# An adaLN transformer block: k-times-v product placed between q products, row sums as two rounded matmuls, three more unread matmuls in the opening

## The chip, the cores and the metric

The kernel runs on one NeuronCore of a Trainium2 chip. The metric is the device time of one execution in microseconds; the median of several executions is compared. A profile is one execution recorded by the hardware profiler.

The engines carry these names in the profile: PE is TensorE (PEld its weight loads), DVE is VectorE, ACT is ScalarE, POOL is GpSimd, and SP issues the DMAs.

## The reference

The input is `x` of 2048 rows by 512 columns, in float32. One row `c` of 512 makes six modulation vectors. A linear-attention block and a bilinear gated block follow, each on a normalised and modulated input and each added back with a gate.

```python
mod = (silu(c) @ w_mod).reshape(1, 6, 1, 512)
sa, ca, ga, sb, cb, gb = six rows of mod
h = layernorm(x) * (1 + ca) + sa
q, k, v = h @ wqkv, 32 heads of 16
pq, pk = phi(q), phi(k)                    # phi(t) = (t > 0 ? t + 1 : exp(t)) + 1e-6
kv = sum over s of pk[s] (outer) v[s]      # one 16 x 16 block per head
z  = sum over s of pk[s]
o  = (pq @ kv) / (pq . z + 1e-6)
x  = x + ga * (o @ wo)
h  = layernorm(x) * (1 + cb) + sb
x  = x + gb * (((h @ w_gate) * (h @ w_up)) @ w_down)
```

## The kernel before

**Precision.** A product of two float32 matrices is made of three matmuls in the type F32R: each operand is split into a rounded high part (a copy on ScalarE) and the rest as a low part (a subtraction on VectorE or GpSimd), and high x high, high x low and low x high are added in PSUM. `split` and `split_raw` make the parts (lines 192 to 194), `product` issues the three matmuls (lines 206, 207 and 208).

**Order.** The schedule is written by hand: each engine gets its instructions in the order in which the code calls them. The 2048 rows are 16 token tiles of 128 rows, in four chunks of four. PSUM has four accumulator banks (`acc_bank`) and four working banks (`bank`); a working bank is given to a new tile when its last reader is done with it.

**The opening (to about 27 us).** The first chunk of `x` is loaded, its statistics are taken, the tiles are normalised and transposed (`transpose_token`, line 278), and two modulation vectors are computed. `keep_on(n)` (line 153) issues n matmuls into the bank `ps_idle` that nobody reads; 18 stand at the start and 2 between the transposes of token tiles 0 and 1. `block_pe` (line 388) and `block_one` (line 399) are the small sums of the modulation.

**k tiles (27 to 129 us).** For each token tile i a loop makes a k product (`proj(i + 2, wk)`), its phi, its split, and adds its products with the normalised input into the four accumulators `tacc` (`t_tile`, lines 355 to 357). `zacc` adds up phi(k) over the tiles on VectorE (`z_add`, line 340). The table `extra` puts further work behind single tiles: the splits of the v weights `wv`, the modulation vectors (`mod_part`, lines 169 and 171; `mod_col`, line 176; `mod_row`, line 186), the loads and splits of `wo`. `mod_row` sums a vector over the 128 partitions and spreads the sum over all rows: one F32 matmul with a 128 x 128 matrix of ones. It is called behind tile 11 (row 2, `ga`) and behind tile 15 (row 5, `gb`). In tile 15 the same matmul makes `zb` from `zacc` (line 654).

**The turn (125 to 157 us).** The accumulators are turned into kv. The eight steps on VectorE are, for each of four k: `n` (line 739), then the low part (line 194), with the high part on ScalarE between them. Then 48 matmuls of 128 columns multiply the v weights with them:

```python
kvps = bank()
for g in range(KD):
    a, b = g * P, (g + 1) * P
    product(kvps[:, a:b], [(cut(wv[k], a, b), cut(tt[k], a, b)) for k in range(KD)])
```

Around them stand q products (`proj(i, wq)`, 12 matmuls of 512 columns each), whose phi is `q_a` (two ScalarE steps, lines 310 and 311) and `q_b` (a maximum and addition on VectorE, line 314). The result is masked to the heads' blocks (line 757), split, and multiplied with `wo` in `w_out` (four groups of three matmuls; the product with `ga` is line 725, and its split follows). Beside it run the denominators: `den_p` (phi(q) times zb, line 676, on POOL or VectorE), `den_r` (sum over a head, line 682), `den_b` (addition and reciprocal, lines 691 and 692), `den_c` (scaling of phi(q), line 711).

**y and the second block (157 us to the end).** `turn_a(i)` transposes the scaled phi(q) (line 782), `turn_h` and `turn_l` split it (lines 786 and 790), and `y_a` multiplies it with the combined weights (line 807). The second block then runs as a stream of matmuls (lines 970 and 1048 to 1050).

Of the kernel before, what the change touches and what calls it, by code (L numbers as in the profile page):

```python
# [8 lines left out]
F32 = mybir.dt.float32  # L9
# [13 lines left out]
def tile_adaln_block(  # L23
# [50 lines left out]
    def B(tag, shape=(P, D), dt=F32):  # L74

        return T(tiles, tag, shape, dt)
# [4 lines left out]
    def bank():  # L81
        return T(ps_w, "bank")
# [1 line left out]

    ident = consts.tile([P, P], F32, name="ident")
    make_identity(nc, ident)
    ones = consts.tile([P, P], F32, name="ones")
    nc.gpsimd.memset(ones, 1.0)
    mask = consts.tile([P, P], F32, name="mask")
    nc.gpsimd.memset(mask, 1.0)  # L90
    m3 = mask.rearrange("p (b i) -> p b i", i=DH)
# [16 lines left out]
    def load(src, tag):  # L108
        raw = B(tag, (P, *src.shape[1:]))[:src.shape[0]]
        nc.sync.dma_start(raw, src)  # L110
        return raw
# [47 lines left out]
    def silu():  # L159
        nc.scalar.activation(ce, ct, AF.Exp, scale=-1.0)  # L160
        nc.vector.tensor_scalar(ce, ce, 1.0, None, op0=ALU.add)
        nc.vector.reciprocal(ce, ce)
        nc.vector.tensor_mul(sc, ct, ce)
# [9 lines left out]
    def mod_col(acc, ps):  # L173

        for b in range(KD):
            nc.tensor.matmul(ps[:, b:b + 1], acc[:, b * P:(b + 1) * P], ones[:, 0:1], start=True, stop=True)
        return ps

    def col_out(v, ps, add):
        t = consts.tile([P, KD], F32, name=f"col{v}")  # L180
        nc.vector.tensor_scalar(t, ps[:, :KD], add, None, op0=ALU.add)
        return t

    def mod_row(v, acc):
        ps = bank()
        nc.tensor.matmul(ps, ones, acc, start=True, stop=True)
        t = consts.tile([P, D], F32, name=f"row{v}")
        nc.scalar.activation(t, ps, AF.Copy)
        return t


    def split(src, h, l, low=None):
        nc.scalar.activation(h, src, AF.Copy)
        (low or nc.vector).tensor_tensor(l, src, f32(h), op=ALU.subtract)

    def split_raw(raw, shape=(P, D), low=None):
        h = B("w", shape, F32R)
        l = B("w", shape, F32R)
        split(raw, h[:raw.shape[0]], l[:raw.shape[0]], low)
        return h, l  # L200

    def product(ps, pairs):

        n = len(pairs)
        for i, ((ah, al), (bh, bl)) in enumerate(pairs):
            nc.tensor.matmul(ps, ah, bh, start=i == 0, stop=False)  # L206
            nc.tensor.matmul(ps, ah, bl, start=False, stop=False)  # L207
            nc.tensor.matmul(ps, al, bh, start=False, stop=i == n - 1)  # L208

    def product2(pss, pairs):  # L210

# [10 lines left out]
    def cut(pair, a, b):  # L222
        return pair[0][:, a:b], pair[1][:, a:b]
# [77 lines left out]
    def proj(i, w, of=bank):  # L301

        ch, j = divmod(i, NJ)
        ps = of()
        product(ps, [(cut(norm[ch].t[k], j * P, (j + 1) * P), w[k]) for k in range(KD)])
        return ps
# [29 lines left out]
    def z_add(i):  # L336
        if i == 1:
            nc.vector.tensor_tensor(zacc, phk[0], phk[1], op=ALU.add)
        elif i > 1:
            nc.vector.tensor_tensor(zacc, zacc, phk[i], op=ALU.add)  # L340
        phk.pop(i - 1, None)
# [22 lines left out]
    def q_b(i):  # L364
        phi_b(q_ps.pop(i), phq[i])
# [16 lines left out]
    def sums_in(b):  # L382
        return ps_idle if b == 1 else ps_m

    def block_pe(v, b):
        at, ps = at_of(v, b), sums_in(b)
        for k, raw in enumerate(half_of(v, b)):
            nc.tensor.matmul(ps[:, at:at + 1], raw, sc[:, k:k + 1], start=k == 0, stop=k == KD - 1)
# [3 lines left out]
    def half_dve(v, half, *ks):  # L392
        if 0 in ks:
            sums[v, half] = B("f")[:, :D // 2]
        mod_acc(sums[v, half], [raw_half[v, half][k // 2][:, k % 2] for k in range(KD)], ks)

    def block_one(v, b):
        at = at_of(v, b)
        nc.tensor.matmul(sums_in(b)[:, at:at + 1], sums[v, b // 2][:, b % 2 * P:(b % 2 + 1) * P], ones[:, 0:1],
                         start=True, stop=True)  # L400

    def block_out(b):
# [38 lines left out]

    keep_on(18)
    n0.stats(0)
    silu()
    n0.stats(1)
    n0.rstd_of(0, 2)
# [10 lines left out]
    keep_on(2)  # L457
    n0.transpose_token(1)
    block_pe(1, 0)
    half_dve(0, 0, 0, 1, 2, 3)  # L460
    weight_h(0)
    n0.transpose_token(2)
    n0.transpose_token(3)
    block_one(0, 0)
    block_out(0)
    weight_l(0)
# [77 lines left out]
    def mod_load(*vs):  # L544
        raw_m.update({v: load_mod(v) for v in vs})

    def mod_part(v, *ks):
        if 0 in ks:
            accs[v] = B("f")
        mod_acc(accs[v], raw_m[v], ks)  # L550
# [4 lines left out]
             7: lambda: (wv.extend(split_raw(r) for r in raw_v[3:4]),),  # L555
             8: lambda: (mod_part(2, 0, 1), mod_load(3)),
             9: lambda: (mod_part(2, 2, 3), mod_load(4)),
             10: lambda: (mod_part(3, 0, 1, 2), mod_load(5)),
             11: lambda: (mod_part(3, 3), mod_part(4, 0, 1), rows.update({2: mod_row(2, accs[2])})),
             12: lambda: (raw_o.extend(load(wo_v[k], "raw") for k in range(KD)), mod_part(4, 2, 3), cols.update({3: col_out(3, mod_col(accs[3], bank()), 0.0)})),  # L560
             13: lambda: (mod_part(5, 0, 1, 2), cols.update({4: col_out(4, mod_col(accs[4], bank()), 1.0)})),
             14: lambda: (mod_part(5, 3), wo_s.extend(split_raw(x) for x in raw_o)), 15: lambda: rows.update({5: mod_row(5, accs[5])})}
    q_at = {4: 3}
    ahead = {}

# [46 lines left out]
    for i in range(4, NT):  # L612
        ch, j = divmod(i, NJ)
        more = ch + 1 < NCH
        if i > 1:
            ahead[i + 2] = proj(i + 2, wk) if i + 2 < NT else proj(i + 6 - NT, wq)
        if i in q_at:
            qps = proj(q_at[i], wq)
        if i + 1 < NT:
            k_split_x(i + 1)  # L620
        if i + 1 < NT:
            k_split(i + 1)
        if more and j < 2:
            t_tile(i, 0, 1)
            nx.transpose(2 * j, 2 * j + 1)
            nx.modulated(ca, sa, 2 * j, 2 * j + 1, cast=nc.vector)
            norm[ch + 1:] = [nx]
        if ch + 2 < NCH and j == 1:
            nx2 = Norm(xts[ch + 2])
            nx2.stats(0, 1)  # L630
        if ch + 2 < NCH and j == 2:
            nx2.stats(2, 3)
            nx2.rstd_of()
        if ch + 2 < NCH and j == 3:
            nx = nx2
            nx.xhat(2)
        if i + 2 < NT:
            k_phi(i + 2, ahead.pop(i + 2))
        else:
            q_a(i + 6 - NT, ahead.pop(i + 2))  # L640
            q_b(i + 6 - NT)
        if i in q_at:
            q_a(q_at[i], qps)
            q_b(q_at[i])
        if i + 1 < NT:
            z_add(i + 1)
        if ch + 2 < NCH and j == 2:
            nx2.nmr_of()
            nx2.xhat(0, 1)
        if ch + 2 < NCH and j == 3:  # L650
            nx.xhat(3)
        if i == NT - 1:
            zps = bank()
            nc.tensor.matmul(zps, ones, zacc, start=True, stop=True)
            zb = consts.tile([P, D], F32, name="zb")
            nc.scalar.activation(zb, zps, AF.Identity, bias=eps_z)  # L656
        t_tile(i, *range(2 if more and j < 2 else 0, KD))
        if i in extra:
            extra[i]()
# [24 lines left out]
    def den_a(ch, *js, on=None):  # L684

        for j in js:
            den_p(ch, j, on=on)
            den_r(ch, j)
# [44 lines left out]
    den_a(0, 0, 1, on=nc.vector)  # L733
    ps = proj(6, wq)
    fs, tt = [], []
    for k in range(KD):
        f = B("n")
        nc.scalar.activation(f, tacc[k], AF.Copy, scale=ca[:, k:k + 1])
        nc.vector.scalar_tensor_tensor(f, zb, sa[:, k:k + 1], f, op0=ALU.mult, op1=ALU.add)
        fs.append(f)  # L740
    for f in fs:
        tt.append((B("w", dt=F32R), B("w", dt=F32R)))
        split(f, *tt[-1])
    q_a(6, ps)
    q_tile(7)
    kvps = bank()
    for g in range(KD):
        a, b = g * P, (g + 1) * P
        product(kvps[:, a:b], [(cut(wv[k], a, b), cut(tt[k], a, b)) for k in range(KD)])
    q_b(6)  # L750
    q_b(7)
    den_p(1, 2)
    den_a(0, 2, on=nc.vector)
    ps = proj(8, wq)
    kvp = (B("xh", dt=F32R), B("xl", dt=F32R))
    kvf = B("n")
    nc.vector.tensor_tensor(kvf.rearrange("p (g c) -> p g c", g=KD), kvps.rearrange("p (g c) -> p g c", g=KD),
                            mask.unsqueeze(1).to_broadcast([P, KD, P]), op=ALU.mult)
    den_p(0, 3, on=nc.vector)
    split(kvf, *kvp)  # L760
    den_r(0, 3)
    den_b(0)
    q_a(8, ps)
    ps = proj(9, wq)
    q_b(8)
    w_out(0, 1)
    q_a(9, ps)
    den_c(0, 1)
    w_out(2, 3)
    q_b(9)  # L770
    q_tile(10)


    pqs = {}
# [322 lines left out]
        return [lambda: den_p(ch, j)], [lambda: den_r(ch, j)]  # L1097

    turn_a(0)
    ps = proj(11, wq)  # L1100
    turn_h(0)
    turn_l(0)
    y_seed(0)
    q_a(11, ps)
# [171 lines left out]
```

## Time and profile before

| what | value |
|---|---|
| median of 3 runs | 561.61 us (560.68 to 561.68) |
| the profiled execution's own time | 561.47 us |
| its span | 559.8 us |
| PE, DVE, ACT, POOL busy | 99%, 68%, 53%, 37% |
| DMA, mean over the span | 102 GB/s |

The span is the time from the first to the last recorded instruction; the profiled execution's own time holds what lies around it. In rows of the chain and of the timeline the first number is the start in us and the second the duration, both from the span's start. A bracket behind a row names the idle time ahead of it and what ended it. Busy times of PE overlap, since matmuls are pipelined: a row that shows 0.39 is followed 0.23 later by the next.

### The profile page before, as it was taken

Reading aid. Unit: us, or ns where it says so; the run is one execution under the profiler, and the core shown is the slowest. Engines: PE = TensorE matmul, PEld = TensorE weight load, DVE = VectorE, ACT = ScalarE, POOL = GpSimd, SP = SyncE. Lnnn points to the kernel's source line nnn. Section 1 sums busy time; section 2 is a strip of 40 time slices with the busy share of each in tenths; the row PEclk is TensorE's granted clock in tenths of the full one; section 3 lists DMA queues with packets and bytes.
Section 4 is the critical chain, followed back from the end, with each engine's and each line's share of the span. In section 5 each row is a group of like instructions: output and inputs, shape, how many; then the busy total and the mean of one; then the engine's idle time right before and its main releaser. Section 6 shows DMA issues by size and latency. Waiting matters only on the chain.

```text
span 559.8 us, 7391 instructions
## 1 busy us (share of the span) xinstructions
PE 551.9 (99%) x2544; PEld 453.5 (81%) x2544; DVE 379.8 (68%) x648; ACT 294.2 (53%) x531; POOL 207.4 (37%) x226
## 2 busy tenths in 40 slices
PE   7999999999999999999999999999999999999997
PEld 5888888888888888888888888878888888888775
DVE  5968779869898998865655766862455545444653
ACT  3876858446476877663545355553444334334420
POOL 2000000003327646343556644485424455554200
PEclk9999999999999999999999999999999999999999
DMA  8910224202230020151446136598353211200004
GB/s 254 384 39 1 75 76 150 77 0 71 80 114 2 0 76 0 39 159 68 150 151 195 32 122 221 178 363 286 114 157 87 57 39 48 71 0 1 0 1 150
DMA packets 50133, 57.24 MB, mean 102 GB/s; under 512 B 6384, under 2 KB 28912, under 8 KB 50096
## 3 DMA queue, kind: packets, MB, share of 16 engines
q1 hardware_dynamic: 50096, 56.77, 31.8%
q8 instruction: 20, 0.33, 0.3%
q14 instruction: 17, 0.14, 0.1%
HBM read 43.12 MB, written 13.63 MB: 101 GB/s over the span
## 4 chain that ended last, share of the span: by engine, by line
PE 94%; DVE 3%; DMA 1%; SPq 0%; issue 0%; ACT 0%; POOL 0%
PE bank L970 38%; PE acc L807 8%; PE acc L1048 7%; PE acc L1049 7%; PE acc L1050 7%; PE bank L206 5%; PE bank L207 5%; PE bank L208 5%; PE acc L357 2%; PE acc L355 2%; PE acc L356 2%; PE bank L271 2%; PE acc L439 1%; DMA x<-in_A_x_dram 1%; PE bank L782 1%; PE acc L271 1%
## 5 line engine op out<-in xcount | busy, mean ns | idle before, releaser
L970 PE MATMUL bank<-h,w 128*128 128x512 f32 (+1 forms) x924 | 215.8, 390 | 0.0
L970 PEld LDWEIGHTS bank<-h,w 128*128 128x128 f32 (+1 forms) x924 | 170.8, 185 | 38.6 <-issue 0.4
L976 ACT ACTIVATE bank<-bank 128x512 f32<-128x512 f32 (+1 forms) x44 | 25.6, 581 | 151.2 <-PE bank L970 151.1
L956 POOL TENSOR_TENSOR w<-raw,w 128x256 fp32r<-128x256 f32 (+3 forms) x44 | 46.1, 1048 | 157.2 <-ACT w L949 150.0
L996 DVE TENSOR_TENSOR phi<-bank,g 128x512 f32<-128x512 f32 (+1 forms) x22 | 15.1, 688 | 83.5 <-PE bank L970 79.8
L1048 PE MATMUL acc<-w,kh 128*128 128x512 f32 (+1 forms) x176 | 68.6, 390 | 0.0
L1049 PE MATMUL acc<-w,kh 128*128 128x512 f32 (+1 forms) x176 | 68.6, 390 | 0.0
L1050 PE MATMUL acc<-w,kl 128*128 128x512 f32 (+1 forms) x176 | 68.5, 389 | 0.0
L956 POOL TENSOR_TENSOR w<-t,w 128x512 fp32r<-128x512 f32 (+1 forms) x44 | 57.4, 1305 | 0.0
L1055 DVE TENSOR_TENSOR x<-acc,x 128x512 f32<-128x512 f32 x80 | 50.3, 681 | 8.6 <-PE acc L1050 8.6
L206 PE MATMUL bank<-w,h 128*128 128x512 f32 x112 | 44.8, 400 | 0.0
L208 PE MATMUL bank<-w,h 128*128 128x512 f32 x112 | 43.7, 390 | 0.0
L207 PE MATMUL bank<-w,h 128*128 128x512 f32 x112 | 43.6, 390 | 0.0
L676 POOL TENSOR_TENSOR f<-h,zb 128x512 f32<-128x512 f32 x12 | 17.1, 1439 | 67.8 <-ACT zb L656 49.2
L249 POOL TENSOR_TENSOR rstd<-ve,half 128x4 f32<-128x4 f32 (+3 forms) x12 | 11.2, 930 | 83.0 <-DVE ve L246 71.4
L807 PE MATMUL acc<-w,xh 128*128 128x512 f32 x128 | 40.7, 399 | 0.0
L1048 PEld LDWEIGHTS acc<-w,kh 128*128 128x128 f32 (+1 forms) x176 | 33.0, 188 | 7.1
L1050 PEld LDWEIGHTS acc<-w,kl 128*128 128x128 f32 (+1 forms) x176 | 33.0, 188 | 7.0
L1049 PEld LDWEIGHTS acc<-w,kh 128*128 128x128 f32 (+1 forms) x176 | 33.1, 188 | 6.9
L938 POOL TENSOR_TENSOR t<-raw,t 128x256 f32<-128x256 f32 (+1 forms) x44 | 36.9, 838 | 1.7
L1022 DVE TENSOR_TENSOR g<-bank,u 128x512 f32<-128x512 f32 (+1 forms) x22 | 15.2, 691 | 27.0 <-ACT u L976 27.0
L264 ACT ACTIVATE n<-x,nmr,rstd 128x512 f32<-128x512 f32 x31 | 23.7, 808 | 14.6 <-DVE nmr L254 14.4
(159 smaller groups left out, 1011.3 us busy)
## 6 DMA issues: line engine op xcount, KB each, us to landing
x<-in_A_x_dram SPq DMA_DIRECT2D x24, 256.0 KB, 5.2
raw<-in_w_mod_dram SPq DMA_DIRECT2D x24, 256.0 KB, 3.8
raw<-in_B_w_gate_dram SPq DMA_DIRECT2D x40, 128.0 KB, 3.0
raw<-in_B_w_up_dram SPq DMA_DIRECT2D x40, 128.0 KB, 3.1
raw<-in_B_w_down_dram SPq DMA_DIRECT2D x20, 256.0 KB, 3.1
side_s<-h SPq DMA_DIRECT2D x16, 256.0 KB, 2.5
h<-side_s SPq DMA_DIRECT2D x16, 256.0 KB, 5.5
out_dram<-x SPq DMA_DIRECT2D x16, 256.0 KB, 2.6
```

Of the source, the lines that this page charges most:

```text
L206: nc.tensor.matmul(ps, ah, bh, start=i == 0, stop=False)
L207: nc.tensor.matmul(ps, ah, bl, start=False, stop=False)
L208: nc.tensor.matmul(ps, al, bh, start=False, stop=i == n - 1)
L807: nc.tensor.matmul(yps[i], x, y, start=fresh and k + n == 0, stop=k == KD - 1 and n == 2, skip_group_check=True)
L938: sub = lambda out, x, y: (on or nc.gpsimd).tensor_tensor(out, x, y, op=ALU.subtract)
L956: sub = lambda out, x, y: (on or nc.gpsimd).tensor_tensor(out, x, f32(y), op=ALU.subtract)
L970: mm = lambda x, y, **kw: nc.tensor.matmul(ps, x[:, k], y, skip_group_check=True, **kw)
L976: nc.scalar.activation(out, x, AF.Copy)
L1048: nc.tensor.matmul(dn[j], hh[:n, a:b], dh[:n], start=i == 0, stop=False)
L1049: nc.tensor.matmul(dn[j], hh[:n, a:b], dl[:n], start=False, stop=False)
L1050: nc.tensor.matmul(dn[j], hl[:n, a:b], dh[:n], start=False, stop=i == n_of - 1)
L1055: nc.vector.tensor_tensor(xt, dn[j], xt, op=ALU.add)
```

## The change

Three things are changed.

1. **Row sums.** `ones` keeps one column, and a new matrix `ones_r` holds ones in F32R. A row sum is two F32R matmuls over a split operand (`over_rows`) instead of one F32 matmul. The operands are split ahead of time: `accs[2]` behind tile 10, `accs[5]` behind tile 13, `zacc` in tile 14. To that end `mod_part(5, 0)` moves to tile 12, `mod_part(5, 3)` to tile 13, and one of the four `wo` splits to tile 13.
2. **The turn.** The eight VectorE steps are interleaved, so that the parts of the first k are ready before the last `n`. The product goes k by k into an accumulator bank: k = 0 and 1 behind q product 7, k = 2 and 3 behind q product 8. The q products behind it, the denominators and the `w_out` groups change places; q product 11 is cut in two around the first transposes of y.
3. **The opening.** One unread matmul is added ahead of the transposes of token tiles 2 and 3, and two behind them.

```diff
+    ones_r = consts.tile([P, P], F32R, name="ones_r")
...
-    def mod_row(v, acc):
+    def over_rows(ps, pair):
+        for m, x in enumerate(pair):
+            nc.tensor.matmul(ps, ones_r, x, start=m == 0, stop=m == 1)
+
+    def mod_row(v, pair):
         ps = bank()
-        nc.tensor.matmul(ps, ones, acc, start=True, stop=True)
+        over_rows(ps, pair)
...
     n0.stats(0)
+    nc.vector.tensor_copy(ones_r, ones.to_broadcast([P, P]))
     silu()
...
     block_pe(1, 0)
+    keep_on(1)
     half_dve(0, 0, 0, 1, 2, 3)
     weight_h(0)
     n0.transpose_token(2)
     n0.transpose_token(3)
+    keep_on(2)
     block_one(0, 0)
...
-             10: lambda: (mod_part(3, 0, 1, 2), mod_load(5)),
+             10: lambda: (accs.update({2: split_raw(accs[2])}), mod_part(3, 0, 1, 2), mod_load(5)),
...
+        if i + 1 == NT - 1:
+            zpair = split_raw(zacc)
...
-            nc.tensor.matmul(zps, ones, zacc, start=True, stop=True)
+            over_rows(zps, zpair)
...
+    def tt_high(k):
+        f = fs[k]
+        nc.vector.scalar_tensor_tensor(f, zb, sa[:, k:k + 1], f, op0=ALU.mult, op1=ALU.add)
+        tt.append((B("w", dt=F32R), B("w", dt=F32R)))
+        nc.scalar.activation(tt[k][0], f, AF.Copy)
+
+    def tt_low(k):
+        nc.vector.tensor_tensor(tt[k][1], fs[k], f32(tt[k][0]), op=ALU.subtract)
+
+    def kv_part(*ks):
+        for k in ks:
+            for g in range(KD):
+                a, b = g * P, (g + 1) * P
+                (ah, al), (bh, bl) = cut(wv[k], a, b), cut(tt[k], a, b)
+                for n, (x, y) in enumerate(((ah, bh), (ah, bl), (al, bh))):
+                    nc.tensor.matmul(kvps[:, a:b], x, y, start=k + g + n == 0, stop=k == KD - 1 and n == 2,
+                                     skip_group_check=True)
...
+    for k in range(KD):
+        tt_high(k)
+        if k:
+            tt_low(k - 1)
+    tt_low(KD - 1)
     q_a(6, ps)
     q_tile(7)
-    kvps = bank()
-    for g in range(KD):
-        a, b = g * P, (g + 1) * P
-        product(kvps[:, a:b], [(cut(wv[k], a, b), cut(tt[k], a, b)) for k in range(KD)])
+    kvps = acc_bank()
+    kv_part(0, 1)
     q_b(6)
     q_b(7)
     den_p(1, 2)
-    den_a(0, 2, on=nc.vector)
     ps = proj(8, wq)
+    den_a(0, 2, 3, on=nc.vector)
+    kv_part(2, 3)
     kvp = (B("xh", dt=F32R), B("xl", dt=F32R))
...
-    den_p(0, 3, on=nc.vector)
     split(kvf, *kvp)
-    den_r(0, 3)
-    den_b(0)
     q_a(8, ps)
     ps = proj(9, wq)
     q_b(8)
+    den_b(0)
+    q_a(9, ps)
     w_out(0, 1)
-    q_a(9, ps)
-    den_c(0, 1)
+    q_b(9)
+    ps = proj(10, wq)
+    den_c(0)
+    q_a(10, ps)
     w_out(2, 3)
-    q_b(9)
-    q_tile(10)
+    ps = bank()
+    pairs = [(cut(norm[2].t[k], 3 * P, 4 * P), wq[k]) for k in range(KD)]
+    product(ps, pairs[:2], end=False)
...
     turn_a(0)
-    ps = proj(11, wq)
+    product(ps, pairs[2:], begin=False)
     turn_h(0)
+    den_c(1)
     turn_l(0)
```

More of the change, by code (lines that the diff above doesn't have):

```diff
@@ L86, in tile_adaln_block @@
     make_identity(nc, ident)
-    ones = consts.tile([P, P], F32, name="ones")
+    ones = consts.tile([P, 1], F32, name="ones")
     nc.gpsimd.memset(ones, 1.0)
+    ones_r = consts.tile([P, P], F32R, name="ones_r")
     mask = consts.tile([P, P], F32, name="mask")
@@ L175, in mod_col @@
         for b in range(KD):
-            nc.tensor.matmul(ps[:, b:b + 1], acc[:, b * P:(b + 1) * P], ones[:, 0:1], start=True, stop=True)
+            nc.tensor.matmul(ps[:, b:b + 1], acc[:, b * P:(b + 1) * P], ones, start=True, stop=True)
         return ps
@@ L200, in split_raw, with product @@
         return h, l
-    def product(ps, pairs):
+    def product(ps, pairs, begin=True, end=True):
         n = len(pairs)
         for i, ((ah, al), (bh, bl)) in enumerate(pairs):
-            nc.tensor.matmul(ps, ah, bh, start=i == 0, stop=False)
+            nc.tensor.matmul(ps, ah, bh, start=begin and i == 0, stop=False)
             nc.tensor.matmul(ps, ah, bl, start=False, stop=False)
-            nc.tensor.matmul(ps, al, bh, start=False, stop=i == n - 1)
+            nc.tensor.matmul(ps, al, bh, start=False, stop=end and i == n - 1)
     def product2(pss, pairs):
@@ L398, in block_one @@
         at = at_of(v, b)
-        nc.tensor.matmul(sums_in(b)[:, at:at + 1], sums[v, b // 2][:, b % 2 * P:(b % 2 + 1) * P], ones[:, 0:1],
+        nc.tensor.matmul(sums_in(b)[:, at:at + 1], sums[v, b // 2][:, b % 2 * P:(b % 2 + 1) * P], ones,
                          start=True, stop=True)
@@ L557, in tile_adaln_block @@
              9: lambda: (mod_part(2, 2, 3), mod_load(4)),
-             10: lambda: (mod_part(3, 0, 1, 2), mod_load(5)),
+             10: lambda: (accs.update({2: split_raw(accs[2])}), mod_part(3, 0, 1, 2), mod_load(5)),
              11: lambda: (mod_part(3, 3), mod_part(4, 0, 1), rows.update({2: mod_row(2, accs[2])})),
-             12: lambda: (raw_o.extend(load(wo_v[k], "raw") for k in range(KD)), mod_part(4, 2, 3), cols.update({3: col_out(3, mod_col(accs[3], bank()), 0.0)})),
-             13: lambda: (mod_part(5, 0, 1, 2), cols.update({4: col_out(4, mod_col(accs[4], bank()), 1.0)})),
-             14: lambda: (mod_part(5, 3), wo_s.extend(split_raw(x) for x in raw_o)), 15: lambda: rows.update({5: mod_row(5, accs[5])})}
+             12: lambda: (raw_o.extend(load(wo_v[k], "raw") for k in range(KD)), mod_part(4, 2, 3), mod_part(5, 0), cols.update({3: col_out(3, mod_col(accs[3], bank()), 0.0)})),
+             13: lambda: (mod_part(5, 1, 2, 3), wo_s.extend(split_raw(x) for x in raw_o[:1]), accs.update({5: split_raw(accs[5])}), cols.update({4: col_out(4, mod_col(accs[4], bank()), 1.0)})),
+             14: lambda: (wo_s.extend(split_raw(x) for x in raw_o[1:]),), 15: lambda: rows.update({5: mod_row(5, accs[5])})}
     q_at = {4: 3}
@@ L735, in tile_adaln_block @@
     fs, tt = [], []
-    for k in range(KD):
[L737 to L743, printed above, removed]
+    def tt_high(k):
[13 more added lines that the diff above has]
+                                     skip_group_check=True)
+    for k in range(KD):
+        fs.append(B("n"))
+        nc.scalar.activation(fs[k], tacc[k], AF.Copy, scale=ca[:, k:k + 1])
+    for k in range(KD):
[3 more added lines that the diff above has]
+    tt_low(KD - 1)
     q_a(6, ps)
     q_tile(7)
-    kvps = bank()
-    for g in range(KD):
-        a, b = g * P, (g + 1) * P
-        product(kvps[:, a:b], [(cut(wv[k], a, b), cut(tt[k], a, b)) for k in range(KD)])
+    kvps = acc_bank()
+    kv_part(0, 1)
     q_b(6)
```

## The prediction

> **What bounds the kernel now.** I read the page's shares first, then the chain that ended last.
>
> ```profile
> span 559.8 us, 7391 instructions
> PE 551.9 (99%) x2544; PEld 453.5 (81%) x2544; DVE 379.8 (68%) x648; ACT 294.2 (53%) x531; POOL 207.4 (37%) x226
> PE 94%; DVE 3%; DMA 1%; SPq 0%; issue 0%; ACT 0%; POOL 0%
> ```
>
> TensorE is busy for 99% of the span and carries 94% of the chain, so time falls only where a TensorE slot gets shorter or a wait of TensorE goes. The 3% on DVE say that in one place another engine is last. The list of waits says where TensorE stands still after its first matmul (line, releaser, us in total, times, longest):
>
> ```profile
> PE bank L278 <- ACT n L264: 1.0, 2, 0.6
> PE acc L399 <- DVE f L171: 0.6, 1, 0.6
> PEld bank L207 <- DVE w L194: 0.4, 2, 0.2
> ```
>
> The first two are in the opening, the third is in the k-times-v product (kv). The chain around that product (start, us, engine, tile, line):
>
> ```profile
> 125.61 0.24 PE bank L208
> 125.87 0.61 ACT h L310
> 126.50 0.64 ACT h L311
> ...
> 132.13 2.65 DVE n L739 x4
> 134.78 2.42 DVE w L194 x4
> 137.25 0.33 PE bank L207
> ```
>
> When q product 5 has ended at 125.85, the chain leaves TensorE and runs 11.4 us through ScalarE and VectorE, back into kv. TensorE has other work meanwhile and loses only the 0.4 above. But VectorE stays nearly full behind it (busy us in two stretches of 4):
>
> ```profile
> 136.00:140.00 4.00, 3.90 (x33) 3.62 (x32) 3.97 (x6) 1.71 (x3) 2.13 (x2) 1.00 0.92 231
> 148.00:152.00 4.00, 4.00 (x19) 3.34 (x18) 3.98 (x7) 2.38 (x4) 0.63 (x1) 1.00 0.04 15
> ```
>
> The columns behind the stretch are PE, PEld, DVE, ACT and POOL, then the granted clock (1.00). TensorE has 3.90 and 4.00 of 4, VectorE 3.97 and 3.98: two engines are near their limit here, and what TensorE saves it can keep only as far as VectorE follows.
>
> **Row sums (L186 twice, L654).** One F32 matmul with `ones`, shown as two instructions, becomes two F32R matmuls.
>
> ```profile
> 103.98 0.86 PE bank L186 x2
> 104.84 0.23 PE bank L206
> 129.30 1.02 PE L186 MATMUL bank<-f,ones 128*128 128x512 f32 x2
> ```
>
> The F32 pair holds the chain for 0.86; an F32R matmul of the same shape holds it for 0.23. The second L186 pair is busy for 1.02, with the overlap of its neighbours; I take all three alike (L654 has the same shape). Each saves 0.86 - 0.46 = 0.40, three save 1.2. [...]
>
> Three roundings are added (one ScalarE copy, one VectorE subtraction each) and a cast of `ones`. The roundings fall between tiles 10 and 15, where VectorE still pauses in each tile:
>
> ```profile
> 115.33 0.69 DVE L314 SCALAR_TENSOR_TENSOR phi<-bank,phi 128x512 f32<-128x512 f32 x1 [2.38 <-ACT phi L311]
> 122.33 0.68 DVE L340 TENSOR_TENSOR z<-z,phi 128x512 f32<-128x512 f32 x1
> 127.16 0.69 DVE L314 SCALAR_TENSOR_TENSOR h<-bank,h 128x512 f32<-128x512 f32 x1 [1.08 <-ACT h L311]
> ```
>
> Pauses of 2.38 and 1.08 hold 0.6 each; I take nothing. The z sum is tightest: `zacc` is complete at 123.0 (122.6 with row 2's saving ahead of it), a copy and a subtraction of 0.6 each follow by 123.9, and TensorE asks when q product 5 ends, at 125.85 - 0.4. If those 1.5 us of cover were gone, TensorE would pay the two steps, 1.2. The cast stands in VectorE's pause ahead of the second statistics (below). The moved `mod_part` calls stay inside the same pauses.
>
> **Unread matmuls.** One goes ahead of the transposes of token tiles 2 and 3, two behind them.
>
> ```profile
> 6.08 0.69 DVE L237 BATCH_NORM_STATS2 st<-x 128x6 f32<-128x512 f32 x1 [0.81 <-DMA x<-in_A_x_dram]
> 11.94 1.09 PE L278 MATMUL bank<-ident,n 128*128 128x128 f32 x8 [0.45 <-ACT n L264]
> 13.58 0.35 PE L399 MATMUL acc<-ones,f 128*128 128x1 f32 x2 [0.56 <-DVE f L171]
> ```
>
> TensorE idles 0.45 and 0.56 in these two places, waiting for `n` and `f`; one matmul (0.23) fits in the first, two (0.46) in the second. I take 0. They cost up to 3 x 0.23 = 0.7 if the idle time were gone. A gain by a faster clock is not there to be had: the granted clock stands at 1.00 of full speed in the stretches shown, and the opening's two pauses are short.
>
> **kv between q products.** The 48 matmuls of 128 columns stay. In the built order 24 of them (k = 0 and 1) follow q product 7, then comes q product 8, then the other 24, then q product 9: the change does what it says.
>
> ```profile
> 135.64 0.22 PE L206 MATMUL bank<-w,w 128*128 128x128 f32 x1
> ...
> 141.43 0.28 PE L208 MATMUL bank<-w,w 128*128 128x128 f32 x1
> 141.54 0.45 PE L206 MATMUL bank<-w,h 128*128 128x512 f32 x1
> 141.83 0.40 PE L207 MATMUL bank<-w,h 128*128 128x512 f32 x1
> ...
> 156.36 0.71 PE L807 MATMUL acc<-w,xh 128*128 128x512 f32 x2
> ```
>
> They start every 0.11 (141.43 to 141.54), so 48 need 5.33; they took 141.54 - 135.64 = 5.90. The waiting, 0.57, goes: the first half needs its second low part only 1.3 us after its start, the second half has q product 8 (12 x 0.23 = 2.7) as cover. The change from 128 to 512 columns costs 0.29 instead of 0.23 and happens once more: 0.06. So TensorE alone would reach the first y matmul (156.36) earlier by 1.2 + 0.57 - 0.06 = 1.7, at 154.65.
>
> **Does VectorE follow?** Its rows of this stretch, with one of ScalarE and one of POOL:
>
> ```profile
> 138.38 1.32 DVE L676 TENSOR_TENSOR f<-h,zb 128x512 f32<-128x512 f32 x1
> 141.74 0.69 DVE L757 TENSOR_TENSOR n<-bank,mask 128x512 f32<-128x512 f32 x1 [1.31 <-PE bank L208]
> 143.52 1.22 DVE L194 TENSOR_TENSOR xl<-n,xh 128x512 fp32r<-128x512 f32 x1
> 145.70 0.95 DVE L692 RECIPROCAL den<-den 128x128 f32<-128x128 f32 x1
> 147.93 1.37 DVE L725 TENSOR_TENSOR n<-bank,row 128x512 f32<-128x512 f32 x2 [0.74 <-PE bank L208]
> 149.32 1.38 DVE L194 TENSOR_TENSOR w<-n,w 128x512 fp32r<-128x512 f32 x2
> 150.61 1.29 DVE L711 SCALAR_TENSOR_TENSOR h<-h,den 128x512 f32<-128x512 f32 x2
> 142.47 0.63 ACT L193 ACTIVATE xh<-n 128x512 fp32r<-128x512 f32 x1 [4.72 <-DVE n L757]
> 137.87 2.97 POOL L676 TENSOR_TENSOR f<-h,zb 128x512 f32<-128x512 f32 x2 [7.01 <-DVE h L314]
> ```
>
> Times below are on the clock of before. Only the first row sum lies ahead of 125.61, so the VectorE chain moves by 0.4: its eight steps (2.65 + 2.42, now interleaved, none dropped) end at 136.8 instead of 137.2. The last high part now waits for the fourth `n` (the sixth of the eight steps, 135.5; so 136.1); ScalarE's four q steps behind it (2 x 0.61 + 2 x 0.64) end at 138.6, and the second q maximum (0.6) on VectorE at 139.2. Then come the den products and sums of tiles 2 and 3, now together and ahead of the kv mask: two products of 0.6 (2.42 / 4, as other two-input steps) and two sums of about 0.7 make 2.6, and 0.65 more for each product that runs against POOL (the 1.32 row). One such: 142.5. On TensorE q product 7 ends 1.2 earlier than 135.64, at 134.4, and kv with q product 8 inside it at 134.4 + 5.4 + 2.7 = 142.5 too. Mask 0.69, high part 0.63, low part 0.6 to 1.22: ready at 144.6 to 145.4, I take 145.3. TensorE needs it after q product 9 (2.7) and two matmuls, at 145.7. Before, two q products covered this step; now one does, and the cover is just enough.
>
> Behind the low part VectorE has, in the new order: q maximum 8 (0.6), den (the reciprocal 0.95 and an estimated 0.25 for the addition, 1.2), two `ga` products (1.37), two lows (1.38), q maximum 9 (0.6), den scaling of tile 0 (0.65), two products and two lows again (2.6), den scaling of tile 1 (0.65): 9.05, ending at 154.35. TensorE is asked to wait for three of them: half of q product 11 needs the bank of q maximum 9 (about 150.6, it arrives at 150.6), the transposes of tile 0 need the second pair of products, and those of tile 1 need that last scaling. Four transposes (0.44) later, at 154.8, y starts. That is 0.2 behind what TensorE could do: the gain is 1.5. Each further 0.6 against POOL, and each 0.3 of ScalarE order, comes off it. With none it is 1.7, with one and some queueing 0.75. I take 1.4, nearer to the fewer collisions, because POOL's work here (2.97 and four short sums) hardly moves.
>
> From the second y step on the order of all engines is that of before and the waits list shows none of TensorE, so the gain stays to the end. DMA queues are not moved past anything that TensorE asks for soon: the x reloads issued behind kv wait about 1 us longer and are used much later.
>
> **Sum.** The profiled execution took 561.47, of which 559.8 are the span; the median of three is 561.61, so it is an ordinary run. 561.6 - 1.4 = 560.2. A measurement of this kernel can tell about 0.2% = 1.1 us from no change.
>
> **Rivals.** *VectorE keeps most of it (chance 0.13):* the den work ahead of the kv mask and one ScalarE detour more put y near 155.6 to 156.5. For it: 3.97 of 4 busy at 136 to 140. Against it: VectorE still pauses 1.31 and 0.74 (rows L757, L725). Gain 0 to 0.7: 561.2.
>
> *More than the bound (0.12):* the earlier k half also lets later steps lose small waits, or the opening gains; over 1.7, about 559.5. Against it: no wait of TensorE behind kv is listed.
>
> *Slower by POOL (0.15):* in the new order nine VectorE steps with both inputs in SBUF (two den products, kv low, four weight lows, two scalings) meet POOL's den products and sums. Two rows show what one meeting costs: 1.32 and 1.22 instead of 0.6. Its place is between 138 and 154; it decides once more than three meetings (2.0 us) beyond mine fall on the path, and ends slower by over 0.2% at five: 561.6 - 1.4 + 5 x 0.6 = 563.2. Against it: POOL has no more work here than before. [...]
>
> **Chances.** Forecast case (gain 0.75 to 1.7) 0.60, of which 0.46 are above 1.1. Faster: 0.46 + 0.12 = 0.58. Within 0.2%: 0.14 + 0.13 = 0.27. Slower: 0.15. The range for 8 in 10 leaves out most of the slow case and the end of the third: 559.2 to 562.2.
>
> **What would show it.** Right: each row sum near 0.46; no wait of the kv weights on L194's successor; the first y matmul about 1.4 earlier, with a short wait of the tile 1 transposes for the den scaling. Wrong: TensorE waiting at the output-weight products for the kv low part, at q product 11 for a bank, or over 0.5 at those transposes; the opening's first transposes or `block_one` starting later; long VectorE steps beside POOL.

## The result and the profile after

The changed kernel took 559.68 us (median of 11 executions, 558.34 to 561.1) against 561.68 for the kernel before (11 executions, 560.37 to 564.35). The ratio is 0.9954, 95% interval 0.9939 to 0.9969: 1.7 to 3.4 us faster, 2.6 by the ratio and 2.0 by the medians. The forecast was 1.4 faster, and its range ended at 559.2; the ratio times the 561.61 of the forecast gives 559.0, just past that end. So the direction was right, and the gain was sized too small. The profiled execution of the changed kernel took 558.88, its span 557.2.

The page and the lists of waits of the changed kernel (releaser, us in total, times, longest):

```profile
span 557.2 us, 7398 instructions
PE 550.5 (99%) x2547; PEld 453.3 (81%) x2547; DVE 381.1 (68%) x652; ACT 296.4 (53%) x534; POOL 207.7 (37%) x226
PE 97%; DVE 1%; DMA 1%; issue 0%; ACT 0%; SPq 0%; POOL 0%; POOLq 0%
PE bank L283 <- ACT n L269: 0.5, 1, 0.5
PEld bank L812 <- DVE h L721: 0.5, 1, 0.5
```

The 3% of VectorE in the chain are down to 1%. The wait inside kv is gone, and so are the one for `f` and one of the two for `n` in the opening. A new one has come, of the transposes of y for the den scaling (L812 for L721). The 0.5 listed is that of the weight loads; TensorE itself stands still for about 0.2, since its last matmul ahead of the transposes starts at 152.71 and is done 0.23 later, and they start at 153.13. TensorE's rows of the row sums and of the turn, with the two VectorE rows that it asks for last (the kv low part and the den scaling):

```profile
102.92 0.62 PE L187 MATMUL bank<-w,ones_r 128*128 128x512 f32 x2
103.37 0.39 PE L211 MATMUL bank<-w,h 128*128 128x512 f32 x1
...
133.39 2.79 PE L762 MATMUL acc<-w,w 128*128 128x128 f32 x24
138.85 2.79 PE L762 MATMUL acc<-w,w 128*128 128x128 f32 x24
153.13 0.66 PE L812 MATMUL bank<-ident,h 128*128 128x128 f32 x4
153.55 0.70 PE L837 MATMUL acc<-w,xh 128*128 128x512 f32 x2
...
143.07 1.28 DVE L199 TENSOR_TENSOR xl<-n,xh 128x512 fp32r<-128x512 f32 x1 [0.70 <-ACT xh L198]
152.39 0.68 DVE L721 SCALAR_TENSOR_TENSOR h<-h,den 128x512 f32<-128x512 f32 x1
```

A row sum now lasts 103.37 - 102.92 = 0.45. From the start of kv to the first y matmul it is 153.55 - 133.39 = 20.16, before 156.36 - 135.64 = 20.72: 0.56 less. From there to the end it is 557.2 - 153.55 = 403.65, before 403.44: nothing is gained behind the turn, and 0.2 is lost. The three stretches of 12 product matmuls that hold a row sum (or 24, for row 5) went from 3.62, 3.63 and 6.34 to 3.17, 3.17 and 5.90, so 0.45 + 0.46 + 0.44 = 1.35. That makes 1.35 + 0.56 - 0.2 = 1.7. The span fell by 2.6. The other 0.94 lie in the opening, whose first k products start here, in the changed kernel and in the kernel before:

```profile
10.99 0.48 PE L154 MATMUL acc<-w 128*128 128x512 f32 x1
12.09 0.71 PE L154 MATMUL acc<-w 128*128 128x512 f32 x2
14.06 1.43 PE L444 MATMUL acc<-w,h 128*128 128x512 f32 x5
...
15.00 1.20 PE L439 MATMUL acc<-w,h 128*128 128x512 f32 x4
```

Two profiled executions can't tell whether these 0.94 belong to the unread matmuls (L154) or to the arrival of x. Nor do they show why 4 of the 11 executions before lay above 562.3 and none after. These were the questions for the runs.

### The profile page after: what moved, and what is told of

The parts are those of the page before. It is cut to its first block, busy times and chain, and to the rows that moved or that the text cites. A ratio compares the mean times of both kernels' runs of the same rounds, so it can differ in the third digit from the quotient of the medians.

```text
span 557.2 us, 7398 instructions
## 1 busy us (share of the span) xinstructions
PE 550.5 (99%) x2547; PEld 453.3 (81%) x2547; DVE 381.1 (68%) x652; ACT 296.4 (53%) x534; POOL 207.7 (37%) x226
## 4 chain that ended last, share of the span: by engine, by line
PE 97%; DVE 1%; DMA 1%; issue 0%; ACT 0%; SPq 0%; POOL 0%; POOLq 0%
PE bank L1000 38%; PE acc L837 8%; PE acc L1079 7%; PE acc L1078 7%; PE acc L1080 7%; PE bank L211 5%; PE bank L213 5%; PE bank L212 5%; PE acc L362 3%; PE acc L360 3%; PE acc L361 3%; PE bank L276 2%; PE acc L444 1%; PE bank L812 1%; PE acc L762 1%; DMA x<-in_A_x_dram 1%
```

## The experiments

Each kernel was timed beside the kernel before on the same chip; four chips were used. "Clock" is the mean granted clock of an execution. "Steady" is a clock of 0.998 or more. In the profiles, the 0.001 or 0.002 that steady executions lack lies behind the work: in that of the changed kernel the last product ends at 553.1, and the clock falls to 0.50 at 555.7, ahead of the end at 557.2. The kernel before, in the 101 executions that stood beside these runs, was steady in 22 (median 561.1; 561.1 to 561.5 on each of the chips), lay at 0.996 or 0.997 in 43 (median 562.6), and at 0.991 to 0.995 in 36 (median 564.2). The ratio of "changed, old kv" leaves out its longest execution, 570.39.

| kernel | median, executions | steady: how many, median | ratio to before, interval |
|---|---|---|---|
| unread matmuls alone | 561.49, 12 | 12, 561.5 | 0.9976, 0.9958 to 0.9994 |
| row sums alone | 564.60, 12 | 5, 560.5 | 1.003, 0.9993 to 1.0067 |
| turn alone | 562.00, 12 | 1, 560.85 | 0.9984, 0.9966 to 1.0003 |
| changed, no unread | 561.63, 12 | 3, 559.2 | 0.9973, 0.9951 to 0.9995 |
| changed, again | 560.02, 12 | 11, 559.8 | 0.9956, 0.9937 to 0.9975 |
| changed, old kv | 564.35, 12 | 5, 561.4 | 1.0001, 0.9973 to 1.0028 |
| changed, old kv filled | 561.87, 12 | 11, 561.9 | 0.9989, 0.9971 to 1.0007 |
| changed, two unread | 559.37, 12 | 10, 559.3 | 0.9955, 0.9935 to 0.9974 |
| changed, F32 row sums | 561.25, 12 | 12, 561.25 | 0.9971, 0.9954 to 0.9987 |
| changed, two in front, two behind | 559.59, 6 | 6, 559.6 | 0.9939, 0.9922 to 0.9956 |
| changed, two in front, all three | 559.95, 6 | 6, 559.95 | 0.9944, 0.9927 to 0.9961 |
| two in front, two behind, scaling early | 560.71, 9 | 9, 560.7 | 0.9954, 0.9933 to 0.9976 |

**Unread matmuls alone.**

```diff
     block_pe(1, 0)
+    keep_on(1)
...
     n0.transpose_token(3)
+    keep_on(2)
     block_one(0, 0)
```

> The kernel before with the three unread matmuls alone. Theory (the gain is row sums 1.35 us and the turn 0.6; the 0.9 by which the changed kernel's profiled execution left the opening earlier is the arrival of x in that one execution): no change, ratio 0.9995 to 1.0005; the first q product starts within 0.2 of where it started before (27.52) once the shift of the second statistics' start is taken off. Rival (the unread matmuls shorten the opening): 0.7 to 0.9 us faster, ratio near 0.9985, and the first q product starts near 26.6 whatever the arrival of x. My second rival: they cost their own 0.7 us, ratio 1.0012.

It was 1.3 faster by the ratio, and all 12 executions were steady, within 560.81 to 562.41, where the kernel before ran from 560.45 to 565.68. The theory (no change) does not hold, and the first rival is not shown: its 0.9985 lies within the interval, and the profile starts the first q product at 26.89 instead of 27.52, but executions of one kernel differ by more than that (26.58 and 28.16 in the changed kernel), and steady executions are no faster. Against those of the kernel before (561.1) the three seem to cost 0.4; with 12 against 22 executions that spread over 2 us, this is rough. What they bring is that no execution lost clock.

**The turn alone** (all of the diff between the VectorE steps of the turn and q product 11; F32 row sums, no unread matmuls).

> The kernel before with the kv halves between q products and the steps moved with it, alone. Theory: the wait inside kv goes, 0.57, less 0.06 for the change of width and up to 0.2 at the transposes of tile 1: 0.4 to 0.55 faster, ratio 0.9990 to 0.9993. Rival (the turn gives more than its list of waits showed, since the measured ratio of the whole change is larger than the sum of 1.35 and 0.6): 1.2 or more faster, ratio under 0.998. Rival of the prediction (VectorE becomes last): 0 or slower, with waits of TensorE at q product 11 or the transposes of tile 1 over 0.5.

Only 1 of 12 executions was steady, 9 lay at 0.995 to 0.997 and 2 at 0.994, so the median tells little of the turn. Its profile has 156.62 - 136.51 = 20.11 from kv to the first y matmul, 0.61 less than before and a little over the theory's 0.55. And it shows what was lost instead. Busy us by engine (PE, PEld, DVE, ACT, POOL), then the granted clock:

```profile
7.67:11.09 3.42, 3.42 (x24) 2.96 (x22) 1.62 (x6) 2.36 (x4) 0.70 (x1) 1.00 1.04 354
11.09:14.50 3.41, 2.36 (x20) 2.10 (x20) 2.77 (x8) 1.75 (x3) 0.00 (x0) 1.00 1.09 363
14.50:17.91 3.41, 3.41 (x11) 2.73 (x11) 3.27 (x9) 3.39 (x7) 0.00 (x0) 0.50 1.07 386
17.91:21.33 3.42, 3.42 (x20) 2.95 (x19) 2.31 (x7) 0.59 (x2) 0.00 (x0) 1.00 1.03 383
```

Behind a stretch in which TensorE is busy for 2.36 of 3.41 us, with transposes and one-column matmuls, the clock stands at 0.50 for 3.41 us and then returns. Half speed for 3.41 us loses 1.7; 1.7 of 560 is the clock of 0.997, and the 43 executions of the kernel before around 0.997 are 1.5 above its steady ones. Two such stretches are 0.994, three 0.991. The longest wait of TensorE ahead of it was 0.56 us.

**Row sums alone.**

```diff
-        nc.tensor.matmul(ps, ones, acc, start=True, stop=True)
+        over_rows(ps, pair)
...
-            nc.tensor.matmul(zps, ones, zacc, start=True, stop=True)
+            over_rows(zps, zpair)
```

> The kernel before with the row sums as two rounded matmuls alone; the turn and the opening as before. Theory: each row sum takes 0.45 less, 1.35 in all, if VectorE follows; the first and the z sum lie ahead of the VectorE chain of the turn, which moves by 0.45 only, so the wait of the kv weights on the low part grows from 0.4 by up to 0.9 and a part is lost: 0.5 to 1.35 faster, ratio 0.9976 to 0.9991. Rival (the sums as the prediction sized them, 0.40 each, and all of it kept): 1.2 faster, 0.9979, with the kv wait unchanged.

The five steady executions gained about 0.5 (560.5 against 561.1), the lower end of the theory. But 7 of 12 were not steady, 6 of those from 0.985 to 0.990 and 566 to 569 us, and the median was 2 us slower, though the interval of the ratio still holds 1. The clock falls in two places, the opening and kv:

```profile
11.66:15.07 3.41, 3.03 (x22) 2.62 (x21) 2.77 (x9) 2.57 (x4) 0.00 (x0) 1.00 1.08 364
15.07:18.48 3.41, 3.41 (x10) 2.66 (x9) 3.30 (x8) 2.51 (x5) 0.00 (x0) 0.50 1.05 387
18.48:21.90 3.42, 3.42 (x21) 2.94 (x20) 1.49 (x5) 1.40 (x3) 0.00 (x0) 1.00 1.06 387
...
134.55:137.95 3.40, 2.74 (x20) 2.18 (x18) 3.40 (x6) 2.86 (x5) 0.26 (x1) 1.00 0.84 215
137.95:141.36 3.41, 3.41 (x19) 3.41 (x18) 2.25 (x3) 0.00 (x0) 3.38 (x3) 0.50 0.31 88
141.36:144.77 3.41, 3.41 (x16) 3.41 (x17) 0.19 (x1) 0.00 (x0) 2.10 (x3) 0.50 0.00 0
144.77:148.19 3.42, 3.42 (x9) 2.65 (x9) 3.25 (x6) 0.63 (x1) 0.00 (x0) 0.50 0.52 164
148.19:151.60 3.41, 3.41 (x16) 2.79 (x16) 1.07 (x2) 1.24 (x2) 0.32 (x1) 1.00 0.43 144
```

The two falls are 137.95 - 15.07 = 122.88 apart, 36.0 times 3.413 (a third of 10.24): in this profile both lie on one grid. In the profile of the changed kernel without unread matmuls, below, the fall behind the last product lies on such a grid too: it comes 158.0 such stretches after the clock's return in the opening. Where the grid lies against the kernel differs between the profiles: the falls in the opening start at 14.50 in the turn alone, 15.07 here and 12.46 in that kernel. Here is why kv is hit. Its first matmul and the second, which waits for the low part:

```profile
134.47 0.22 PE L211 MATMUL bank<-w,w 128*128 128x128 f32 x1
135.20 0.33 PE L212 MATMUL bank<-w,w 128*128 128x128 f32 x1 [0.51 <-DVE w L199]
```

The shorter row sums bring TensorE to kv earlier, but the eight VectorE steps ahead of it move less. The waits of the kv weights grow from 0.4 to 1.3 in all, and only some 20 matmuls fall into a stretch of 3.41 us. Then the clock stands at half for 10.24 us: it did not return while the 128-column matmuls left to do ran, to 144.34, and returned at 148.19, behind the first stretch of 512-column matmuls. That loses 5 us.

**The changed kernel without its unread matmuls.**

```diff
-    keep_on(1)
...
-    keep_on(2)
     block_one(0, 0)
```

> The changed kernel without the three unread matmuls. Theory: the same as the changed kernel by the terms of the turn and the row sums, 1.7 to 1.9 faster than before, ratio 0.9966 to 0.9970; the waits on n and f in the opening are back. Rival (unread matmuls give the rest): the same 1.8 here, while the unread matmuls alone give 0.7 to 0.9; the two ratios multiplied give 0.9954. Under the theory the runs of the kernel alone show no gain, and the whole change's 0.9954 lies 0.6 above its terms by the spread of the runs of the kernel before.

By the ratio it is 1.5 faster than before, with 9 of 12 executions not steady, down to 0.991. Its three steady ones have a median of 559.2. Turn and row sums together are worth 561.1 - 559.2 = 1.9 where no clock is lost, the 1.35 + 0.56 of the traces; the unread matmuls take about 0.4 to 0.6 of it back (559.7 and 559.8 with them, against three executions without), and keep the clock. Its profile lost 10.24 us in the opening, from 12.46 to 22.70, behind a wait of 0.89.

**The changed kernel, once more.**

> The changed kernel, once more, beside the three that follow. Clock theory: no stretch of half clock in any execution, so the mean granted clock of every one is 0.998 or more, all times within about 1.5 us of each other, near 559.7. Rival (the spread is chance of the chip and not the kernel's): some executions at 0.997 to 0.991 and up to 564.

Eleven of 12 were steady; one, against the theory, lay at 0.991 and 564.33. The profiled execution shows that a wait need not sink the clock, and that the opening's times vary by chance:

```profile
9.19 0.66 PE L283 MATMUL bank<-ident,n 128*128 128x128 f32 x4 [1.27 <-ACT n L269]
12.56 1.09 PE L283 MATMUL bank<-ident,n 128*128 128x128 f32 x8 [0.54 <-ACT n L269]
15.62 0.74 PE L444 MATMUL acc<-w,h 128*128 128x512 f32 x2
```

TensorE waited 1.27 and 0.54 here, and the clock was 0.999. The same kernel starts its k products at 15.62 in this execution and at 14.06 in the one of the result: the 0.94 between the two profiles of the result are within what one kernel shows.

**Old kv in the changed kernel, and the same with its wait filled.** The first has row sums and unread matmuls, and kv as one train. The second adds:

```diff
     kvps = bank()
+    for _ in range(6):
+        nc.tensor.matmul(kvps, idle[:, :P], idle, start=True, stop=True)
     for g in range(KD):
```

> Row sums and unread matmuls, with the 48 kv matmuls in one train as before. Clock theory: the opening keeps its clock, but kv starts 0.9 earlier than before against a VectorE chain that moves by 0.45 only; its waits thin the 128-column matmuls to some 20 in a stretch of 3.41 us, and about half of the executions lose 10.24 us at half clock there: two groups, near 560.3 at 0.999 and near 565 to 566 at 0.991, none at 0.997. Rival (VectorE's lateness costs its waits and no clock; what the row sums alone lost came from the opening): one group, 560.2 to 560.8, all at 0.999.

> The kernel of the run before it with six unread matmuls of 512 columns ahead of kv, into the bank that kv then overwrites: they take the 1.36 us in which kv would wait for its low parts. Clock theory: no half clock in kv any more, one group near 560.3 at 0.999, so the six cost nothing and save the 5 us of the slow half. Rival (the long train of 128-column matmuls sinks the clock by its shape, waits or not): still two groups, the upper near 565. Second rival (fill costs its time): 561.7, one group.

With the old kv there were two groups: five steady executions (median 561.4) and seven from 0.982 to 0.993 with a median of 565.4. The profile is of the second group. Its clock falls in kv alone, from 136.31 to 146.55, 10.24 us again, behind a stretch in which TensorE is busy for 2.76 of 3.41 us with 18 matmuls:

```profile
137.95:141.36 3.41, 3.41 (x18) 3.41 (x17) 1.01 (x2) 0.00 (x0) 3.33 (x4) 0.50 0.02 6
```

With six matmuls more, 11 of 12 were steady at 561.9, and one lay at 0.994. In the filled kernel the stretches at the same times as above are:

```profile
134.51 1.52 PE L758 MATMUL bank<-w 128*128 128x512 f32 x6
...
134.55:137.95 3.40, 3.40 (x25) 3.10 (x24) 3.40 (x7) 2.89 (x6) 0.23 (x1) 1.00 0.65 164
137.95:141.36 3.41, 3.41 (x33) 3.41 (x32) 2.28 (x3) 0.00 (x0) 3.41 (x3) 1.00 0.56 147
141.36:144.77 3.41, 3.41 (x17) 2.83 (x16) 3.11 (x5) 1.08 (x2) 3.11 (x4) 1.00 0.49 144
```

An unbroken train of 33 small matmuls kept the clock at 1.00 (32 in the stretch of this execution's own grid, 136.08 to 139.49); the thinned one of some 20 lost it. So here it is the wait within the train and not the shape of its matmuls alone. The fill seems to cost 0.5 in steady executions, less than the 1.36 that it takes; with five steady ones to compare with, that is rough.

**Only two unread matmuls** (no `keep_on(1)`).

> The changed kernel with only the two unread matmuls behind the transposes of tiles 2 and 3, without the one ahead of them. Clock theory: between the kernel with none (9 of 12 executions with a clock under 0.998) and with three (none of 11): one third or less of the executions with 3.41 us at half clock, the others 0.1 to 0.2 faster than with three; median 559.5 to 560. Rival (only the first is needed, since the 0.45 ahead of the transposes is what starves the clock): as with none, median over 561.

The share is as expected, and the rival is out: 10 of 12 steady; the other two at 0.996 and 0.992. The steady ones lie at 559.3, 0.4 to 0.5 below the kernel with three, where 0.1 to 0.2 was expected. The median is no worse than with three.

**F32 row sums in the changed kernel.**

> The changed kernel with the row sums as single F32 matmuls, as before. Theory: no execution loses clock in kv, at most one in the opening; 1.35 slower than the changed kernel, 561.0 to 561.2, and 0.4 to 0.6 faster than the kernel before with the unread matmuls alone (561.5). Rival (row sums and the turn each give a part only together): the turn alone gives nothing beside the unread matmuls, 561.5.

All 12 were steady at 561.25, 1.45 above the changed kernel, for the 1.35 of the trace. That completes four combinations with a steady clock and the unread matmuls: neither 561.5, the turn 561.25, the row sums 561.4, both 559.8 (559.68 in the result). By these medians, from three chips and with five executions for the row sums, each alone gives 0.1 to 0.25, less than expected of the turn; both give 1.7 to 1.8. The trace is sharper on the turn:

```profile
135.43 2.79 PE L754 MATMUL acc<-w,w 128*128 128x128 f32 x24
155.54 0.70 PE L829 MATMUL acc<-w,xh 128*128 128x512 f32 x2
```

From kv to y that is 20.11, so the turn alone gives 20.72 - 20.11 = 0.61. The row sums alone give 1.35 less the 0.9 by which the waits in kv grow, about 0.45. Both give 1.9. The parts do not add up: shorter row sums alone hand most of what they save to the wait in kv, and the turn removes that wait.

**Fill where TensorE waits anyway** (`keep_on(18)` becomes `keep_on(20)`; the first without, the second with the one ahead of the transposes).

> The changed kernel with two more unread matmuls in its first train (20 in place of 18), where TensorE waits 0.2 to 1.3 us for the first n, and none ahead of the transposes of tiles 2 and 3; the two behind them stay. Theory (they fill a wait there and cost nothing; more activity ahead of the thin stretch keeps the clock): undisturbed executions near 559.3 as with the two alone, at most one of 12 under 0.998, median 559.3 to 559.6. Rival (the thin stretch is that of the transposes from 9 to 15 us, which the front doesn't fill): as with the two alone, 2 of 12 or more under 0.998. Second rival (the front is on the path): 0.45 slower, 559.8.

> The changed kernel with all of its three unread matmuls and two more in the first train. Theory: no execution of 12 under 0.998; undisturbed executions as the changed kernel, 559.7. Rival (front on the path): 560.1. It tells with the first run what the one ahead of the transposes costs: 0.4 by the runs so far.

All 12 executions of the two were steady, at 559.6 and 559.95. The first has the best ratio of all, 0.9939, but its interval overlaps the changed kernel's, so it isn't shown to be the better one. Six executions also can't tell it from the kernel with two, nor show whether the longer first train costs time.

**The den scaling of tile 1 earlier**, the wait that the new list shows.

```diff
     q_a(10, ps)
+    den_c(1)
     w_out(2, 3)
...
     turn_h(0)
-    den_c(1)
     turn_l(0)
```

> The kernel with two unread matmuls in front and two behind the transposes, and the den scaling of tile 1 ahead of the second pair of output-weight products instead of behind it. Theory (the 0.2 to 0.3 that TensorE waits ahead of tile 1's transposes is the forecast's last VectorE term and all that VectorE costs): that wait goes, the first y matmul comes 0.2 to 0.3 earlier against the start of kv (20.16 in the changed kernel, so 19.9), median 559.3, clock 0.998 or more in at least 11 of 12. Rival (the scaling only changes place with the products: the banks that the second pair reads are freed 0.6 later and TensorE waits for a bank, or for the low parts in y): as many waits elsewhere, no gain or 0.3 slower.

The rival was right in its mechanism, and the price was higher than its 0.3. TensorE, VectorE and POOL in its profile:

```profile
153.72 0.66 PE L812 MATMUL bank<-ident,h 128*128 128x128 f32 x4 [0.93 <-DVE n L734]
155.96 0.73 PE L837 MATMUL acc<-w,xh 128*128 128x512 f32 x2
...
150.67 2.39 DVE L720 SCALAR_TENSOR_TENSOR h<-h,den 128x512 f32<-128x512 f32 x2
...
150.90 1.62 POOL L685 TENSOR_TENSOR f<-h,zb 128x512 f32<-128x512 f32 x1 [3.02 <-DVE h L319]
```

The two scalings take 2.39 beside POOL's product instead of about 1.2, the second pair of products comes later, and the transposes of tile 0 wait 0.93 for it. Kv started at 134.91, so the first y matmul came after 21.05 instead of 20.16. The times point the same way, 560.71 against 559.59 for the kernel that it was built from, but on two chips, and the intervals of the ratios overlap.

That kernel's own profile (two in front, two behind) was an exception in the turn, too: 20.85 from kv to y, where the other profiles of the new turn, without the early scaling, have 20.11 to 20.17. There a den product on VectorE took 1.85 beside POOL instead of 0.68 at 127.83, the eight steps ended 0.8 later, and kv waited for its low parts. It was the longest of six executions, 560.68.

## Why the prediction was right and where it was not

**What bounds the kernel: right. The sum of row sums and turn: 0.5 short.** TensorE alone could reach y 1.7 earlier and VectorE would take 0.2 to 0.3 of it, the forecast said. In the trace the row sums gave 1.35 (sized 1.2) and kv to y 0.56 (sized 0.57 less 0.06 less 0.2 to 0.3, so 0.2 to 0.3). The difference in the second is a wait that the full list of the kernel before holds and that the sum left out:

```profile
PEld bank L782 <- DVE n L725: 0.3, 1, 0.3
```

There the transposes of tile 0 waited for the second pair of output-weight products; every kernel with the old turn has this wait, and the changed kernel doesn't. Between steady executions the whole change is 561.1 - 559.7 = 1.4, the number of the forecast. That is luck, for two errors cancel: 1.9 instead of 1.4 from turn and row sums, less about 0.5 that the unread matmuls cost.

**Row sums: 0.40 should have been 0.45.** The chain's 0.86 was taken for the whole F32 pair, but the product matmul behind it also lasted 0.80 (at 104.27), where the one behind the new pair lasts 0.39 (at 103.37); the stretch as a whole shows it, with 3.62 against 3.17.

**VectorE: right in place, a little pessimistic in size.** The kv low part came in time (its row ends at 144.35, and no wait for it is listed). The prediction's own rows for it add up to 144.4 to 145.0, and not to the 144.6 to 145.4 that it gave; set on its clock by the start of kv (134.4 there, 133.39 here), the part was ready at 145.4, since its step took 1.28 and small gaps lay between the steps. The wait foretold, of tile 1's transposes for the den scaling, is there, at about 0.2. That the transposes of tile 0 hang on the second pair of products is what the early scaling confirmed, with 0.93.

**Unread matmuls: the step that failed.** "I take 0", since "a gain by a faster clock is not there to be had: the granted clock stands at 1.00 of full speed in the stretches shown". One profiled execution was read as the clock of all. It was a steady one; 79 of 101 executions of that kernel were not. Alone, the three made the kernel 1.3 faster (0.3 to 2.4 by the interval). They cost about 0.4 to 0.6 of the 0.7 that the prediction gave as the dearest case, and they save the 1.5 or 3.1 that a lost stretch or two cost in the other executions. The pauses of 0.45 and 0.56 were called short; with 0.49 and 0.56 in the same places the turn alone lost its clock. The three times known to the forecast, 560.68 to 561.68, did not show this; the later ones, up to 566, do. That, with the 1.9 for 1.4 above, is why the measured gain is above 1.4, and by how much varies with the share of steady executions in the kernel before.

**The rivals.** "More than the bound" named the opening and about 559.5, which is near what was measured, but by smaller waits and not by clock. "Slower by POOL" did not decide the result; the early scaling shows one such meeting, of 1.2 us, and one profiled execution of the new turn lost 0.7 to another. How much of the spread between executions is of this kind is not shown. "VectorE keeps most of it" is what happens to the row sums without the turn: 0.9 of 1.35.

**Open.** What in a stretch decides on a fall isn't settled. By these profiles busy time alone isn't it: 3.03 of 3.41 led to a fall in the opening of the row sums alone, while in the kernel before the stretch from 10.15 to 13.56 was busy for 2.43 and led to none. Where that profile's grid lies is an estimate, 160 times 3.413 us counted back from the fall behind its last product (559.69). One execution of the changed kernel in 23 still lost 0.009 of its clock, in a place that no profile caught. And the clocks of the 11 executions of the kernel before in the result are not on record, so their share of steady ones is taken from the later 101.

## What to carry to other kernels

Look at the mean clock of every execution and not only at the profiled one: the times that stood in steps here (1.5 us for 0.003 of clock) were lost clock, and the place was found in a profile that had it. TensorE waits between small matmuls cost several times their length here (waits of 1.3 in all lost 5 us), so a saving that brings TensorE earlier to such a wait can make the kernel slower until the wait is filled or moved. Parts of a change that share one queue are not to be summed from runs of each alone.

## What the runs showed of the hardware

In these profiles the granted clock fell to 0.50 for 3.41 or 10.24 us, behind stretches thinned by waits of 0.4 to 0.9 us; the two falls of the row sums alone began 36.0 times 3.413 us apart. Not every stretch with such waits led to a fall: with waits of 1.27 and 0.54 the changed kernel, once more, had a clock of 0.999. At half clock the 128-column matmuls follow one another every 0.21 us instead of 0.11 and did not bring the clock back (137.95 to 144.34 in the row sums alone). One stretch of 512-column matmuls did (144.77 to 148.19). Two other profiles show how whole it was: the stretch from 14.50 in the turn alone, where they begin at 14.74, was enough, and the one from 15.87 in the changed kernel without unread matmuls, where they begin at 16.59, was not.

Two VectorE steps of about 0.6 each took 2.39 beside a POOL step of 1.62 (the early scaling); all of these read two inputs from SBUF.
